# Squared-ReLU attention and a gated feed-forward on one core: a planned instruction order, 7-row loads, and crossbar transposes for batches 3 to 7

## The chip, the cores and the metric

The kernel runs on 1 core of a Trainium2 chip. The metric is device time in microseconds (us). A result here is the median of 4 to 7 executions of one kernel. Each kernel ran beside the kernel before, on the same chip in the same rounds; where two changed kernels of different rounds are compared, the kernel before differed by at most 0.4 us between them (505.1 to 505.5 us). TensorE is called PE, VectorE DVE, ScalarE ACT, GpSimd POOL, and the queue that issues stores and crossbar transposes SP. Tiles lie in SBUF; matmuls write theirs to PSUM, from where ACT or DVE copies them out (an eviction) before the PSUM tile can be used again. The granted clock is the share of the full TensorE clock that the profile shows.

## The reference, cut to what matters

```python
batch, n_heads, seq, head_dim = (8, 12, 448, 64)        # q, k, v in float32
n_tokens, d_model, d_ff = (3584, 768, 1536)

def _attn_ref(q, k, v):
    S = q.shape[2]
    scores = scale * np.matmul(q, k.transpose(0, 1, 3, 2))
    attn = np.maximum(scores, 0.0) ** 2 / S
    return np.matmul(attn, v)

def _moe_ref(x, w_gate, w_val, w_out):                  # x: the attention output, 3584 x 768
    gate = np.maximum(x @ w_gate, 0.0)
    val = x @ w_val
    return gate * val @ w_out
```

There is no softmax, so attention is two matmuls with a squared ReLU between them. The scores contract over the head dimension, so PE needs queries and keys with that dimension on the partitions; they arrive with the sequence there and have to be transposed.

## The kernel before

Loads go through POOL, which also casts to bf16. The 448 rows of a head are split into 384 in runs of 3 rows per partition and a tail of 64 single rows. PE transposes two heads at a time, and DVE copies the result out of PSUM:

```python
def load_batch(b, nsplit):                 # nsplit 3 for batches 0 and 1, else 1
    ...
    nc.gpsimd.dma_start(out=km[:, hs], in_=rows_main(k, b, hs))
    nc.gpsimd.dma_start(out=qm[:, hs], in_=rows_main(q, b, hs))
    nc.gpsimd.dma_start(out=tl[ko:ko + TAIL, hs], in_=rows_tail(k, b, hs))
    nc.gpsimd.dma_start(out=tl[qo:qo + TAIL, hs], in_=rows_tail(q, b, hs))
    nc.gpsimd.dma_start(out=vm[:, hs], in_=rows_main(v, b, hs))
    ...                                    # and four small loads of the tail of v

def transpose_pair(b, hp):
    t_ps = psum.tile([128, 2 * S], BF16, name="t_ps", tag="acc", bufs=4)
    for i in range(2 * NC + 1):
        for h2 in range(2):
            ...
            nc.tensor.transpose(t_ps[64 * h2:64 * h2 + 64, i * 128:(i + 1) * 128], blk, ident)
    qk_sb = tpool.tile([128, 2 * S], BF16, name="qk_sb")
    nc.vector.tensor_copy(qk_sb, t_ps)
```

Attention goes by groups of four heads, ten steps each: seven score steps `s`, one product with the values `pv` (of the group before), two transposes `t` (for the group after). Each score step is followed by a ReLU (144 of 168 on ACT, the others on DVE) and a square on DVE. The feed-forward of the batch before is a queue of units (6 or 12 matmuls each), and a running quota puts about one unit between every two attention steps:

```python
for i, s in enumerate(steps):
    s()
    if qd.g == 0 and qd.b > 0 and i == 3:
        ffn_queue.extend(ffn_units(qd.b - 1))
        per = len(ffn_queue) / (NQ * len(steps) - i - 1)
    acc += per
    while acc >= 1.0 and ffn_queue:
        ffn_queue.pop(0)()
        acc -= 1.0
```

The loads stand in the order batch 0, all gate and value weights, batch 1, output weights.

Of the kernel before, what the change touches and what calls it, by code (L numbers as in the profile page):

```python
# [8 lines left out]
FP32 = mybir.dt.float32  # L9
BF16 = mybir.dt.bfloat16  # L10
AF = mybir.ActivationFunctionType
ALU = mybir.AluOpType


@with_exitstack
def kernel(
# [10 lines left out]
    nc = tc.nc  # L27

# [5 lines left out]
    NC = S // 128  # L34
    MAIN = NC * 128
    TAIL = S - MAIN
    assert TAIL == 64 and D == 64
# [5 lines left out]
    WC = 256  # L43
# [6 lines left out]
    inp = ctx.enter_context(tc.tile_pool(name="inp", bufs=3))  # L50
    tpool = ctx.enter_context(tc.tile_pool(name="tpool", bufs=6))
    rpool = ctx.enter_context(tc.tile_pool(name="rpool", bufs=3))
    apool = ctx.enter_context(tc.tile_pool(name="apool", bufs=2))
    xpool = ctx.enter_context(tc.tile_pool(name="xpool", bufs=2))
    hpool = ctx.enter_context(tc.tile_pool(name="hpool", bufs=2))
# [3 lines left out]

    ident = const.tile([128, 128], BF16)  # L60
    make_identity(nc, ident)
# [3 lines left out]
    w_out_sb = wpool.tile([128, KF, d_model], BF16)  # L65

    def load_gv(c):
        cols = slice(c * WC, (c + 1) * WC)
        wg = moe_w_gate.rearrange("(kd p) f -> p kd f", p=128)
        wv = moe_w_val.rearrange("(kd p) f -> p kd f", p=128)  # L70
        nc.gpsimd.dma_start(out=w_gate_sb[c], in_=wg[:, :, cols])
        nc.gpsimd.dma_start(out=w_val_sb[c], in_=wv[:, :, cols])

    def load_out(c, n):
        wo = moe_w_out.rearrange("(kf p) m -> p kf m", p=128)
        s = slice(c * n, (c + 1) * n)
        nc.gpsimd.dma_start(out=w_out_sb[:, s], in_=wo[:, s])
# [3 lines left out]
    def rows_main(x, b, hs):  # L81
        return x[b, hs, 0:MAIN, :].rearrange("h (p t) d -> p h t d", t=NC)

    def rows_tail(x, b, hs):
        return x[b, hs, MAIN:S, :].rearrange("h p d -> p h d")

    batch = {}

    def q_first(b):
        return b % 2 == 0  # L90

    def load_batch(b, nsplit):
        qm = inp.tile([128, H, NC, D], BF16, name="qm")
        km = inp.tile([128, H, NC, D], BF16, name="km")
        tl = inp.tile([128, H, D], BF16, name="tl")
        vm = inp.tile([128, H, NC, D], BF16, name="vm")
        vt = inp.tile([128, NQ, 2, D], BF16, name="vt")
        qo, ko = (0, TAIL) if q_first(b) else (TAIL, 0)
        n = H // nsplit
        for i in range(nsplit):  # L100
            hs = slice(i * n, (i + 1) * n)
            nc.gpsimd.dma_start(out=km[:, hs], in_=rows_main(k, b, hs))  # L102
            nc.gpsimd.dma_start(out=qm[:, hs], in_=rows_main(q, b, hs))  # L103
            nc.gpsimd.dma_start(out=tl[ko:ko + TAIL, hs], in_=rows_tail(k, b, hs))  # L104
            nc.gpsimd.dma_start(out=tl[qo:qo + TAIL, hs], in_=rows_tail(q, b, hs))  # L105
            nc.gpsimd.dma_start(out=vm[:, hs], in_=rows_main(v, b, hs))  # L106

            gs = slice(i * n // 4, (i + 1) * n // 4)
            vq = v[b, hs, MAIN:S, :].rearrange("(g f) p d -> f p g d", f=4)
            nc.gpsimd.dma_start(out=vt[0:64, gs, 0], in_=vq[0])  # L110
            nc.gpsimd.dma_start(out=vt[0:64, gs, 1], in_=vq[3])
            nc.gpsimd.dma_start(out=vt[64:128, gs, 0], in_=vq[1])
            nc.gpsimd.dma_start(out=vt[64:128, gs, 1], in_=vq[2])
        batch[b] = (qm, km, tl, vm, vt)


    def col_offsets(b):
        if q_first(b):
            return 0, S
        return S, 0  # L120

    def transpose_pair(b, hp):
        qm, km, tl, vm, vt = batch[b]
        h0 = 2 * hp
        first, last = (qm, km) if q_first(b) else (km, qm)
        t_ps = psum.tile([128, 2 * S], BF16, name="t_ps", tag="acc", bufs=4)
        for i in range(2 * NC + 1):
            for h2 in range(2):
                h = h0 + h2
                blk = first[:, h, i, :] if i < NC else tl[:, h, :] if i == NC else last[:, h, i - NC - 1, :]  # L130
                nc.tensor.transpose(t_ps[64 * h2:64 * h2 + 64, i * 128:(i + 1) * 128], blk, ident)  # L131
        qk_sb = tpool.tile([128, 2 * S], BF16, name="qk_sb")
        nc.vector.tensor_copy(qk_sb, t_ps)  # L133
        return qk_sb


    def key_cols(b, c):
        if q_first(b):
            return S + TAIL + c * 128
        return c * 128  # L140

    def tail_cols(b):
        return S if q_first(b) else MAIN

    def q_cols(b):
        return slice(0, S) if q_first(b) else slice(S, 2 * S)

    def relu2(s_ps, dst, on_vec):
        src = s_ps[:, :, :S]
        r_sb = rpool.tile([128, 2, S], BF16, name="r_sb")  # L150
        if on_vec:
            nc.vector.tensor_scalar_max(r_sb, src, 0.0)  # L152
        else:
            nc.scalar.activation(r_sb, src, AF.Relu)  # L154
        nc.vector.tensor_tensor(dst, r_sb, r_sb, ALU.mult)  # L155

    xbuf = {}

    class Quad:
        def __init__(self, b, g):  # L160
            self.b, self.g = b, g
            self.qk = {}

        def t(self, j):
            self.qk[j] = transpose_pair(self.b, 2 * self.g + j)

        def s(self, i):
            b = self.b
            if i == 0:
                self.at = apool.tile([128, 7, 2, S], BF16, name="at")  # L170
            s_ps = psum.tile([128, 2, 512], FP32, name="s_ps", tag="s", bufs=2)
            qc = q_cols(b)
            if i < 6:
                qk = self.qk[i // NC]
                kc = key_cols(b, i % NC)
                for h2 in range(2):
                    p = slice(64 * h2, 64 * h2 + 64)
                    nc.tensor.matmul(s_ps[:, h2, :S], lhsT=qk[p, kc:kc + 128], rhs=qk[p, qc],  # L178
                                     start=True, stop=True)
            else:  # L180

                kc = tail_cols(b)
                for j, h2, half in ((0, 0, 0), (0, 1, 1), (1, 0, 1), (1, 1, 0)):
                    p = slice(64 * h2, 64 * h2 + 64)
                    o = slice(64 * half, 64 * half + 64)
                    nc.tensor.matmul(s_ps[o, h2, :S], lhsT=self.qk[j][p, kc:kc + TAIL],  # L186
                                     rhs=self.qk[j][p, qc], start=True, stop=True)
            relu2(s_ps, self.at[:, i], i == 2)

        def pv(self):  # L190
            b, g = self.b, self.g
            qm, km, tl, vm, vt = batch[b]
            x_ps = psum.tile([128, 2, 512], FP32, name="x_ps", tag="s", bufs=2)
            for j in range(2):
                for c in range(NC):
                    for h2 in range(2):
                        o = slice(64 * h2, 64 * h2 + 64)
                        nc.tensor.matmul(x_ps[o, j, :S], lhsT=vm[:, 4 * g + 2 * j + h2, c, :],  # L198
                                         rhs=self.at[:, 3 * j + c, h2, :],
                                         start=(c == 0), stop=False)  # L200
            for j, h2, half in ((0, 0, 0), (0, 1, 1), (1, 0, 1), (1, 1, 0)):
                p = slice(64 * half, 64 * half + 64)
                o = slice(64 * h2, 64 * h2 + 64)
                nc.tensor.matmul(x_ps[o, j, :S], lhsT=vt[p, g, j, :],  # L204
                                 rhs=self.at[p, 6, h2, :], start=False, stop=True)
            if g == 0:
                xbuf[b] = xpool.tile([128, KD, S], BF16, name="xT")
            nc.scalar.copy(xbuf[b][:, 2 * g:2 * g + 2, :], x_ps[:, :, :S])  # L208

    hbuf = {}  # L210

    def ffn_units(b):
        units = []
        if b % 2 == 0:
            hbuf[b // 2] = hpool.tile([128, KF, 2 * S], BF16, name="hT")
        hT = hbuf[b // 2]
        t0 = (b % 2) * S
        xT = xbuf[b]

        st = {}  # L220

        def g_unit(mf):
            def emit():
                c, o = divmod(mf * 128, WC)
                g_ps = psum.tile([128, 512], FP32, name="g_ps", tag="acc", bufs=4)[:, :S]
                for kd in range(KD):
                    nc.tensor.matmul(g_ps, lhsT=w_gate_sb[c][:, kd, o:o + 128], rhs=xT[:, kd, :],  # L227
                                     start=(kd == 0), stop=(kd == KD - 1))
                g_sb = gpool.tile([128, S], BF16, name="g_sb")
                nc.scalar.activation(g_sb, g_ps, AF.Relu)  # L230
                st[mf] = g_sb
            return emit
# [129 lines left out]
```

## Time and profile before

| | before |
|---|---|
| device time, median (range) | 505.3 us (504.5 to 505.86) |
| span of the profiled run | 502.9 us |
| PE busy | 470.9 us, 94% |
| PE busy in the first 50 us | 22.0 us |
| two batches, from the first output unit of one to that of the next but one | 116.4 us |
| interruptions of the feed-forward by attention in those two batches | 58 |

From the page of the kernel before: span, busy times, the rows of PE, its granted clock and the DMA engines in 40 slices (tenths), and the chain of waits that ended last.

```profile
span 502.9 us, 7712 instructions
...
PE 470.9 (94%) x3264; PEld 221.4 (44%) x3264; DVE 210.9 (42%) x336; ACT 224.1 (45%) x321; POOL 90.0 (18%) x130
...
PE   2842999999999999999999999999999999999997
...
PEclk9975999999999999999999999999999999999999
DMA  9999999975092423725092150010001200010002
...
PE 90%; DMA 5%; POOL 4%; issue 0%; ACT 0%; POOLq 0%
```

PE is full from the fifth slice to the last but one, and 90% of the chain that ended last is PE. Only the first 50 us have room. The timeline of PE shows the largest hole there (columns: start, duration, engine, line, operation, count, and in brackets the idle time before it and what ended it):

```profile
34.46 0.38 PE L186 MATMUL s_ps<-qk_sb 64*64 64x448 bf16 x4 [0.44 <-ACT r_sb L154]
47.25 0.85 PE L131 MATMUL t_ps<-ident,km 128*64 128x128 bf16 x12 [12.41 <-DMA km<-in_k_dram]
48.04 0.93 PE L227 MATMUL g_ps<-xT,wg_93 128*128 128x448 bf16 x2
```

PE waits 12.41 us for the keys of batch 1, which are queued behind all gate and value weights. The first feed-forward unit (L227) starts after that, at 48.0 us. The same view in the middle of the kernel:

```profile
229.07 1.31 PE L227 MATMUL g_ps<-xT,wg_93 128*128 128x448 bf16 x6
230.31 0.36 PE L178 MATMUL s_ps<-qk_sb 64*128 64x448 bf16 x2
230.61 1.31 PE L239 MATMUL v_ps<-xT,wv_99 128*128 128x448 bf16 x6
231.85 0.36 PE L178 MATMUL s_ps<-qk_sb 64*128 64x448 bf16 x2
232.15 1.31 PE L227 MATMUL g_ps<-xT,wg_94 128*128 128x448 bf16 x6
233.29 1.30 PE L239 MATMUL v_ps<-xT,wv_100 128*128 128x448 bf16 x6
234.52 0.36 PE L131 MATMUL t_ps<-ident,qm 128*64 128x128 bf16 x6
```

The starts are what to read. Unit L227 at 232.15 is followed by its like at 233.29, 1.14 us later. The unit before a score step holds PE 1.24 us (229.07 to 230.31) and the score step itself 0.30 us (230.31 to 230.61), where a second score step in a row takes 0.195 us. So an interruption of the feed-forward costs about 0.2 us, and there are 28 to 30 in a batch.

### The profile page before, as it was taken

To read this page: it belongs to the slowest core of one execution; us is meant where nothing else is said; L and a number is where in the kernel's file an instruction comes from. 1 tells how busy PE (TensorE), PEld (TensorE's weight loads), DVE (VectorE), ACT (ScalarE), POOL (GpSimd) and SP (SyncE) were. 2 spreads that over 40 slices of the span, in tenths; PEclk is the share of its full clock that TensorE was granted. 3 is DMA by queue.
4 is the path that set the end of the run, shared out by engine and by line. 5 is a ranking of instruction groups with operands and counts; after the bars stand their busy time and mean duration, and the time that the engine had idled before them with its cause. 6 is when DMAs were issued, how large, how long until landed. Compare 5 with 4: busy or idle time off the path is not lost.

```text
span 502.9 us, 7712 instructions
## 1 busy us (share of the span) xinstructions
PE 470.9 (94%) x3264; PEld 221.4 (44%) x3264; DVE 210.9 (42%) x336; ACT 224.1 (45%) x321; POOL 90.0 (18%) x130
## 2 busy tenths in 40 slices
PE   2842999999999999999999999999999999999997
PEld 1411444544445444454445444454445544455554
DVE  1750655335551454535452355515552255521210
ACT  2560555445453555445453454435553455443221
POOL 9944945420110202002020110000000000000000
PEclk9975999999999999999999999999999999999999
DMA  9999999975092423725092150010001200010002
GB/s 94 138 197 168 121 205 186 185 142 53 0 111 64 99 20 36 76 95 56 0 111 64 64 55 2 1 63 33 2 0 33 95 0 1 2 61 34 0 25 101
DMA packets 72161, 35.09 MB, mean 70 GB/s; under 512 B 57792, under 2 KB 68544, under 8 KB 72128
## 3 DMA queue, kind: packets, MB, share of 16 engines
q0 software_dynamic: 68032, 23.60, 42.0%
q1 hardware_dynamic: 4096, 11.01, 6.0%
q8 instruction: 25, 0.41, 0.3%
q14 instruction: 8, 0.07, 0.0%
HBM read 47.19 MB, written 11.01 MB: 116 GB/s over the span
## 4 chain that ended last, share of the span: by engine, by line
PE 90%; DMA 5%; POOL 4%; issue 0%; ACT 0%; POOLq 0%
PE g_ps L227 24%; PE v_ps L239 23%; PE o_ps L256 23%; PE s_ps L178 7%; PE x_ps L198 6%; PE t_ps L131 5%; DMA km<-in_k_dram 3%; DMA wg_95<-in_moe_w_gate_dram 2%; PE x_ps L204 1%; PE s_ps L186 1%; POOL km L102 0%; POOL vm L106 0%; POOL qm L103 0%; POOL tl L104 0%; POOL tl L105 0%; POOL vt L110 0%
## 5 line engine op out<-in xcount | busy, mean ns | idle before, releaser
L155 DVE TENSOR_TENSOR at<-r_sb 128x896 bf16<-128x896 bf16 x168 | 104.1, 624 | 173.5 <-ACT r_sb L154 173.0
L154 ACT ACTIVATE r_sb<-s_ps 128x896 bf16<-128x896 f32 x144 | 129.7, 917 | 64.4 <-PE s_ps L178 53.5
L256 PE MATMUL o_ps<-w_out_sb,hT 128*128 128x384 bf16 x672 | 115.8, 327 | 0.0
L230 ACT ACTIVATE g_sb<-g_ps 128x448 bf16<-128x448 f32 x96 | 52.3, 545 | 84.9 <-PE g_ps L227 84.9
L241 DVE TENSOR_TENSOR hT<-v_ps,g_sb 128x448 bf16<-128x448 f32 x96 | 59.6, 621 | 64.2 <-PE v_ps L239 64.2
L256 PEld LDWEIGHTS <-hT 128*128 128x128 bf16 x672 | 62.7, 98 | 44.8 <-issue 5.0
L260 ACT ACTIVATE o_sb<-o_ps 128x384 f32<-128x384 f32 x56 | 27.5, 491 | 82.5 <-PE o_ps L256 82.5
L178 PE MATMUL s_ps<-qk_sb 64*128 64x448 bf16 x288 | 52.9, 373 | 4.4 <-ACT r_sb L154 2.4
L133 DVE COPY qk_sb<-t_ps 128x896 bf16<-128x896 bf16 x48 | 29.6, 620 | 32.8 <-PE t_ps L131 32.8
L208 ACT CAST xT<-x_ps 128x896 bf16<-128x896 f32 x24 | 21.7, 906 | 43.0 <-PE x_ps L204 43.0
L178 PEld LDWEIGHTS <-qk_sb 64*128 64x128 bf16 x288 | 14.0, 93 | 50.4 <-issue 48.8
L198 PE MATMUL x_ps<-at,vm 128*64 128x448 bf16 x288 | 33.2, 366 | 0.4 <-ACT r_sb L154 0.4
L131 PE MATMUL t_ps<-ident,km 128*64 128x128 bf16 x288 | 19.2, 239 | 12.4 <-DMA km<-in_k_dram 12.4
L106 POOL DMA_DIRECT2D vm<-in_v_dram x12 | 11.0, 917 | 101.4 <-PE x_ps L198 69.7
L131 PE MATMUL t_ps<-ident,qm 128*64 128x128 bf16 x288 | 18.7, 238 | 9.4 <-DMA qm<-in_q_dram 9.4
L152 DVE TENSOR_SCALAR r_sb<-s_ps 128x896 bf16<-128x896 f32 x24 | 26.1, 1086 | 2.9 <-PE s_ps L178 2.9
L239 PE MATMUL v_ps<-xT,wv_99 128*128 128x448 bf16 x96 | 23.7, 358 | 0.0
L227 PE MATMUL g_ps<-xT,wg_93 128*128 128x448 bf16 x96 | 23.4, 363 | 0.0
L198 PEld LDWEIGHTS <-vm 128*64 128x64 bf16 x288 | 16.4, 112 | 14.9 <-issue 8.3
L131 PEld LDWEIGHTS <-km 128*64 128x64 bf16 x288 | 12.0, 119 | 21.7 <-DMA km<-in_k_dram 12.7
L239 PE MATMUL v_ps<-xT,wv_101 128*128 128x448 bf16 x96 | 20.9, 354 | 0.0
L227 PE MATMUL g_ps<-xT,wg_95 128*128 128x448 bf16 x96 | 20.9, 354 | 0.0
(55 smaller groups left out, 408.1 us busy)
## 6 DMA issues: line engine op xcount, KB each, us to landing
out_dram<-o_sb SPq DMA_DIRECT2D x24, 384.0 KB, 2.3
km<-in_k_dram POOLq DMA_DIRECT2D x6, 576.0 KB, 8.1
qm<-in_q_dram POOLq DMA_DIRECT2D x6, 576.0 KB, 9.2
vm<-in_v_dram POOLq DMA_DIRECT2D x6, 576.0 KB, 7.0
w_out_sb<-in_moe_w_out_dram POOLq DMA_DIRECT2D x4, 576.0 KB, 9.1
out_dram<-o_sb SPq DMA_DIRECT2D x8, 192.0 KB, 2.7
km<-in_k_dram POOLq DMA_DIRECT2D x6, 192.0 KB, 3.8
qm<-in_q_dram POOLq DMA_DIRECT2D x6, 192.0 KB, 4.2
```

Source lines behind the costliest of these rows:

```text
L131: nc.tensor.transpose(t_ps[64 * h2:64 * h2 + 64, i * 128:(i + 1) * 128], blk, ident)
L133: nc.vector.tensor_copy(qk_sb, t_ps)
L154: nc.scalar.activation(r_sb, src, AF.Relu)
L155: nc.vector.tensor_tensor(dst, r_sb, r_sb, ALU.mult)
L178: nc.tensor.matmul(s_ps[:, h2, :S], lhsT=qk[p, kc:kc + 128], rhs=qk[p, qc], start=True, stop=True)
L198: nc.tensor.matmul(x_ps[o, j, :S], lhsT=vm[:, 4 * g + 2 * j + h2, c, :], rhs=self.at[:, 3 * j + c, h2, :], start=(c == 0), stop=False)
L227: nc.tensor.matmul(g_ps, lhsT=w_gate_sb[c][:, kd, o:o + 128], rhs=xT[:, kd, :], start=(kd == 0), stop=(kd == KD - 1))
L230: nc.scalar.activation(g_sb, g_ps, AF.Relu)
L239: nc.tensor.matmul(v_ps, lhsT=w_val_sb[c][:, kd, o:o + 128], rhs=xT[:, kd, :], start=(kd == 0), stop=(kd == KD - 1))
L241: nc.vector.tensor_tensor(hT[:, mf, t0:t0 + S], v_ps, st[mf], ALU.mult)
L256: nc.tensor.matmul(o_ps, lhsT=hT[:, kf, ti * 128:(ti + 1) * 128], rhs=w_out_sb[:, kf, hf * OH:(hf + 1) * OH], start=(kf == 0), stop=(kf == ...
L260: nc.scalar.activation(out=o_sb[:, hf * OH:(hf + 1) * OH], in_=o_ps, func=AF.Copy, scale=float(out_scale))
```

## The change

It does four things. It loads q and k in runs of 7 rows (448 = 64 x 7) and v in runs of 4 and 3 of these, so the loads become fewer and longer. It gathers attention into bursts of two or three steps. It replaces the quota by a list schedule: a small planner with assumed durations picks, step by step, what can start next, which decides the order in which the operations are emitted, and it shares PSUM evictions between ACT and DVE. For batches 3 to 7 the transposes leave PE: DVE regroups q and k into pairs of heads (seven copies), and two crossbar DMAs on the SP queue transpose them from SBUF to SBUF. The planner cut to its core, and the parts that matter (lines joined and shortened; batch 0 has its steps in a slightly different order):

```diff
+    tc.manual_schedule(engines={ET.PE, ET.DVE, ET.Activation, ET.Pool, ET.SP})
+XBAR_FROM = 3
+class Op:                     # engines with assumed durations, dependencies, buffers, transfer time
+    def commit(self, op, s, e):                 # (of the planner)
+        self.t[e] = s + d
+        op.end = s + d
+        if op.xfer:
+            if e == "POOL":                     # loads: one queue, one transfer after the other
+                self.dmaq = max(self.dmaq, op.end + 1.0) + op.xfer
+                op.end = self.dmaq + 1.0
+            else:                               # stores and crossbar transposes on SP
+                op.end += 2.0 + op.xfer
+    ...
+    order = sorted(range(len(P.ops)), key=lambda i: (P.ops[i].start, i))
+    return [P.ops[i] for i in order]            # emitted in the order of planned starts
 
+    rows = lambda x: x[b, hs].rearrange("h (p t) d -> p h t d", t=NT)      # NT = 7
+    k_op = dma_in(lambda: tile_of("qk", NT)[64:128, hs], rows(k), 64 * n, 64 * n * 0.06 / 16, alloc=al)
+    q_op = dma_in(lambda: st.qk[0:64, hs], rows(q), 64 * n, 64 * n * 0.06 / 16)
+    v0, v1 = ...                                # the same with 0.045
 
+def transpose_batch(b):                         # batches 3 to 7
+    for s, t in enumerate(slot_order(b)):       # seven copies, on DVE
+        op = Op({"DVE": 0.28}, lambda s=s, t=t: emit_pair(s, t), deps=deps + perm[:1],
+                alloc=[pair] if s == 0 else [], reads=[st.buf])
+    for i in range(2):                          # q, then k: one crossbar DMA each, on SP
+        op = Op({"SP": 0.3}, lambda i=i: emit_x(i), deps=perm + xo[:1], ..., xfer=8.0)
 
+    for c in range(d_ff // WC):                 # batch 1 among the weights
+        load_gv(c)
+        if c % 2 == 0:
+            load_heads(1, 2 * c, 4)
 
+    nb += 1; att.append((qd.s(0), nb)); att.append((qd.s(1), nb))          # a burst
+    nb += 1; att.append((qd.s(2), nb)); PV()
+    nb += 1; att.append((qd.s(3), nb)); att.append((qd.s(4), nb)); T(n + 1)
+    nb += 1; att.append((qd.s(5), nb)); att.append((qd.s(6), nb))
```

For the loads of a whole batch (12 heads) the planner assumes 2.88 us each for k and q and 2.16 us for each half of v: 10.1 us of transfer in all, about 12 us with its two fixed microseconds. PSUM becomes four tiles of two banks that all work shares; there is one buffer `pair` for the regrouped heads and two for the transposed ones.

## The prediction

> **What bounds the kernel now.** TensorE. On the page PE is busy 94% of the 502.9 us span, and the chain of waits that ended last is 90% PE, with 5% DMA and 4% POOL at its start. By windows, PE is busy 100% from 50 us to the last matmul (about 499 us). Before that it loses some 28 us: in 0 to 50 us it is busy 22.0 us, much of that at a lowered clock (granted 0.77 and 0.50 in the two slices from 25 to 50 us, against 1.00 after). The largest hole, 34.8 to 47.3 us, waits for the keys of batch 1, which are queued behind all gate and value weights.
>
> After 50 us the timeline repeats with 116.4 us per two batches, 58.2 us each. Start to start, over four batches: feed-forward about 44 us per batch, scores 2.03 us and PV 1.57 us per group of four heads, transposes 0.545 us per pair of heads (3.3 us per batch). A lone score step takes 0.295 us, the second of two in a row 0.195 us; a gate or value unit takes 1.14 us after its like and 1.235 us where an attention step adjoins. So each interruption of the feed-forward costs about 0.2 us, and there are some 28 per batch. The Trainium skill (TensorEngine Tiling, Key Properties) says that changing the tiling mode drains the array; these differences agree.
>
> **What the change does.**
> 1. Transposes of batches 3 to 7 leave PE: 15 groups x 1.09 us = 16 us, all critical.
> 2. Attention comes in 4 bursts per group instead of about 9.5. My sum for a batch: feed-forward 42.2, scores 5.5, PV 4.7 = 52.4 us without transposes, 55.2 us with them, against 58.2. Five batches save 5.8, two save 3.0: about 35 us, step 1 included.
> 3. Start: fewer, longer DMA runs (12 loads for batch 0 instead of 27, issued at about 0.65 us each), batch 1 interleaved with the weights, evictions shared between ACT and DVE. A group in the start is bound by evictions: 8.8 us on ACT now; about 13.2 us of ACT and DVE work over two engines, so 6.6 us. Feed-forward of batch 0 should begin at about 33 us and PE stay full from there, instead of 47: about 15 us.
> 4. Added: seven DVE regroupings and two crossbar transposes of 0.69 MB per batch on the store queue. The skill (DMA: Bandwidth & Descriptors, Latency) gives 261 GB/s for transposing DMA, hence an estimate of 5 us per batch; nothing in this trace shows it. Against 52 us per batch and loads a batch ahead it is off the path.
>
> Sum: 505 - 35 - 15 = 455, plus about 4 us for imperfect packing.
>
> **Predicted: 459 us, 80% range 447 to 475.** Faster by over 2%: 0.95; within 2%: 0.03; slower: 0.02.
>
> **What would show it.** PE near 100% from about 33 us; no transposes on PE after batch 2; o-to-o period of two late batches near 105 us instead of 116.4; chain still about 90% PE; PE waits after 40 us under 8 us in total; crossbar landing in under 12 us.
>
> **What would make it wrong.** Crossbar transposes taking tens of microseconds, delaying scores or holding stores behind them on the same queue; PSUM tiles shared by both streams making PE wait on relu or square; the start still bound by weights or eviction; idle PE lowering the clock again; the plan's order blocking an in-order engine.

## The result

The change takes 476.16 us (475.33 to 477.61, 4 runs) against 505.3 us before. The ratio is 0.9427 (95% interval 0.9398 to 0.9457). All ratios here are the mean time of one kernel's fast runs over that of the other's of the same rounds, so not quite the ratio of the medians quoted. The direction and most of the mechanism were right, but 459 us was predicted with 475 us as the upper end.

The page of the change, the same rows:

```profile
span 475.9 us, 6835 instructions
...
PE 439.7 (92%) x2844; PEld 217.2 (46%) x2844; DVE 207.2 (44%) x343; ACT 216.8 (46%) x319; POOL 45.6 (10%) x68
...
PE   3769999996999999996999969999999999999995
...
PEclk9899999997999999998999988999999999999999
DMA  9999999997317800793027940079001300021013
...
PE 74%; DMA 17%; DVE 2%; ACT 2%; POOL 2%; issue 2%; SPq 0%; ACTq 0%; DVEq 0%; POOLq 0%
```

PE is full earlier. But there are now dents in its row and in its clock in the middle of the kernel (slices 10, 19 and 24), and the chain that ended last is 17% DMA and only 74% PE; by lines, 13% are loads of queries and 4% key transposes. Three stops of PE explain the dents:

```profile
PE ps L501 <- DVE hT L517: 4.6, 1, 4.6
PE ps L405 <- DVE hT L517: 4.5, 1, 4.5
PE ps L309 <- DVE hT L517: 4.0, 1, 4.0
```

Each time PE waited, by this view, for a DVE multiplication (L517, gate times value, which frees PSUM). The second stop in full: first PE, then DVE, then POOL and SP, which issue the DMAs.

```profile
216.43 1.30 PE L501 MATMUL ps<-xT,wg_99 128*128 128x448 bf16 x6
222.20 0.56 PE L405 MATMUL ps<-qT,kT 64*128 64x448 bf16 x2 [4.47 <-DVE hT L517]
222.69 2.45 PE L451 MATMUL ps<-at,vv 128*64 128x448 bf16 x12
...
225.38 1.31 PE L511 MATMUL ps<-xT,wv_105 128*128 128x448 bf16 x6
```
```profile
212.08 0.63 DVE L517 TENSOR_TENSOR hT<-ps,g_sb 128x448 bf16<-128x448 f32 x1 [0.74 <-ACT g_sb L506]
219.64 1.97 DVE L350 COPY pair<-qk 128x768 bf16<-128x768 bf16 x7 [6.94 <-DMA qk<-in_q_dram]
221.53 0.62 DVE L517 TENSOR_TENSOR hT<-ps,g_sb 128x448 bf16<-128x448 f32 x1
```
```profile
199.66 1.50 POOL L232 DMA_DIRECT2D vv<-in_v_dram  x2 [48.31 <-PE ps L456]
...
201.87 0.80 POOL L232 DMA_DIRECT2D qk<-in_q_dram  x1
```
```profile
199.57 4.14 SPq L362 DMA_TRANSPOSE kT<-pair  x1
```

DVE finishes L517 at 212.7 us. The next instruction in its order is the first regrouping (L350) of batch 6, whose queries are still on their way, so it stands still for 6.94 us. Behind it in the same queue is the multiplication that PE needs. PE still does two score steps and three feed-forward units; its next score step then needs a PSUM tile that this multiplication frees, and PE stops for 4.47 us. The Trainium skill ("TensorE: Matmul & The Clock Gate", Architectural detail, engine queue depths) says ACT and DVE are strict FIFO; the trace agrees: L517 starts the moment the copies end. The copies were in no hurry: the first crossbar transpose of this batch started at 245.4 us, 23.8 us after the last of them. The chain of waits says the same from the other end (start, duration, what):

```profile
199.66 1.31 POOL vv L232 x2
...
201.87 17.70 DMA qk<-in_q_dram
...
219.64 1.97 DVE pair L350 x7
221.61 0.54 DVE hT L517
...
222.20 0.56 PE ps L405 x2
```

The third stop is like the second: DVE waits 6.85 us for queries of batch 7. At the first, the view names the key transpose of batch 3, which was still reading the single buffer `pair` (issued at 91.7 us, landed 18.9 us later, at 110.6). But the queries of batch 4 had landed only at 110.0 us (issued at 89.15 us, 20.8 us to landing), so without the busy buffer DVE would have waited only 0.6 us less:

```profile
91.73 10.41 SPq L362 DMA_TRANSPOSE kT<-pair  x1
110.72 1.97 DVE L350 COPY pair<-qk 128x768 bf16<-128x768 bf16 x7 [6.65 <-DMA kT<-pair]
```

After the stop at 222 us PE runs slowly. The windows of that stop and of what follows give the granted clock as the third number from the end:

```profile
217.70:222.20 4.50, 0.03 (x1) 0.05 (x1) 2.56 (x9) 0.55 (x1) 0.00 (x0) 0.94 0.06 9
222.20:226.40 4.20, 4.20 (x24) 1.70 (x24) 2.17 (x4) 1.81 (x2) 0.00 (x0) 0.66 0.00 0
```

PE gets 0.66 of its clock over the next 4.2 us, so the PV product at 222.69 took 2.45 us where 1.33 us is usual. After the other two stops the clock was 0.51 for 5.6 us and 0.50 for 5.7 us. That agrees with the skill's page just named (Part 1: an idle window of about 3.4 us halves the clock). The three stops cost 3.99 + 4.47 + 4.62 = 13.1 us, and the slow clock after them 5.6 x 0.49 + 4.2 x 0.34 + 5.7 x 0.50 = 7.0 us.

Where nothing stops, the two late batches from 308.4 to 414.0 us took 105.6 us. The prediction had named 105 us as the sign that the bursts and the crossbar work.

### The profile page after: what moved, and what is told of

It is laid out like the page before. It is cut to its first block, busy times and chain, and to the rows that moved or that the text cites. A ratio compares the mean times of both kernels' runs of the same rounds, so it can differ in the third digit from the quotient of the medians.

```text
span 475.9 us, 6835 instructions
## 1 busy us (share of the span) xinstructions
PE 439.7 (92%) x2844; PEld 217.2 (46%) x2844; DVE 207.2 (44%) x343; ACT 216.8 (46%) x319; POOL 45.6 (10%) x68
## 3 DMA queue, kind: packets, MB, share of 16 engines
q0 software_dynamic: 37856, 24.38, 35.8%
q1 hardware_dynamic: 31680, 17.90, 19.8%
## 4 chain that ended last, share of the span: by engine, by line
PE 74%; DMA 17%; DVE 2%; ACT 2%; POOL 2%; issue 2%; SPq 0%; ACTq 0%; DVEq 0%; POOLq 0%
PE ps L542 21%; PE ps L501 20%; PE ps L511 20%; DMA qk<-in_q_dram 13%; PE ps L451 5%; PE ps L405 5%; DMA kT<-pair 4%; PE ps L456 1%; DVE pair L350 1%; PE ps L309 1%; ACT r_sb L426 1%; PE ps L411 1%; POOL qk L232 1%; POOL vv L232 1%; DVE hT L517 1%
## 5 line engine op out<-in xcount | busy, mean ns | idle before, releaser
L426 ACT ACTIVATE r_sb<-ps 128x896 bf16<-128x896 f32 x134 | 117.5, 925 | 8.3 <-PE ps L405 8.3
L506 ACT ACTIVATE g_sb<-ps 128x448 bf16<-128x448 f32 x96 | 52.3, 545 | 138.7 <-PE ps L511 110.0
L517 DVE TENSOR_TENSOR hT<-ps,g_sb 128x448 bf16<-128x448 f32 x96 | 59.8, 624 | 116.5 <-ACT g_sb L506 103.2
L550 ACT ACTIVATE o_sb<-ps 128x384 f32<-128x384 f32 x56 | 25.0, 490 | 79.2 <-PE ps L542 76.2
L542 PE MATMUL ps<-wo_109,hT 128*128 128x384 bf16 x336 | 59.3, 326 | 0.8 <-ACT r_sb L426 0.8
L542 PE MATMUL ps<-wo_110,hT 128*128 128x384 bf16 x336 | 59.2, 326 | 0.3
L428 DVE TENSOR_SCALAR r_sb<-ps 128x896 bf16<-128x896 f32 x34 | 37.1, 1090 | 47.0 <-PE ps L405 38.3
L451 PE MATMUL ps<-at,vv 128*64 128x448 bf16 x288 | 33.2, 368 | 0.4 <-ACT r_sb L426 0.4
L405 PE MATMUL ps<-qT,kT 64*128 64x448 bf16 x180 | 27.1, 362 | 4.5 <-DVE hT L517 4.5
L470 ACT CAST xT<-ps 128x896 bf16<-128x896 f32 x23 | 21.0, 913 | 11.5 <-PE ps L456 11.5
L501 PE MATMUL ps<-xT,wg_99 128*128 128x448 bf16 x96 | 21.9, 366 | 4.6 <-DVE hT L517 4.6
L309 PE MATMUL ps<-ident,qk 128*64 128x128 bf16 x252 | 12.4, 271 | 14.9 <-DMA qk<-in_q_dram 9.8
L501 PE MATMUL ps<-xT,wg_100 128*128 128x448 bf16 x96 | 22.2, 370 | 0.0
L511 PE MATMUL ps<-xT,wv_105 128*128 128x448 bf16 x96 | 22.0, 367 | 0.0
L511 PE MATMUL ps<-xT,wv_106 128*128 128x448 bf16 x96 | 21.6, 362 | 0.1
L501 PE MATMUL ps<-xT,wg_97 128*128 128x448 bf16 x96 | 21.6, 363 | 0.0
L451 PEld LDWEIGHTS <-vv 128*64 128x64 bf16 x288 | 14.9, 112 | 13.8 <-issue 7.0
L511 PE MATMUL ps<-xT,wv_107 128*128 128x448 bf16 x96 | 20.8, 352 | 0.2
L501 PE MATMUL ps<-xT,wg_98 128*128 128x448 bf16 x96 | 20.8, 353 | 0.0
## 6 DMA issues: line engine op xcount, KB each, us to landing
vv<-in_v_dram POOLq DMA_DIRECT2D x12, 384.0 KB, 10.1
qk<-in_q_dram POOLq DMA_DIRECT2D x6, 672.0 KB, 19.2
```

The lines of the kernel that those rows point to most:

```text
L405: nc.tensor.matmul(s_ps[:, h2, :S], lhsT=k_of(h2, key_off(b) + (i % NC) * 128, 128), rhs=q_of(h2), start=True, stop=True)
L426: nc.scalar.activation(loc["r"], loc["s"][:, :, :S], AF.Relu)
L428: nc.vector.tensor_scalar_max(loc["r"], loc["s"][:, :, :S], 0.0)
L451: nc.tensor.matmul(x_ps[o, j, :S], lhsT=st.vv[:, 4 * g + 2 * j + h2, 1 + c, :], rhs=at[:, NC * j + c, h2, :], start=(c == 0), stop=False)
L501: nc.tensor.matmul(loc["g"], lhsT=w_gate_sb[c][:, kd, o:o + 128], rhs=st.xT[:, kd, :], start=(kd == 0), stop=(kd == KD - 1))
L506: nc.scalar.activation(loc["gs"], loc["g"], AF.Relu)
```

## The experiments

My theory after reading the trace (A): the plan's order puts the regroupings in DVE's queue before their data (at the first stop, their buffer too) are there, and an in-order queue makes everything behind them wait. Rival (B): the crossbar traffic, the shared PSUM tiles or the clock cost the time, wherever the regroupings stand. Both regrouping shifts, the kernel without crossbar and the bursts alone ran on one chip together, beside the kernel before (505.1 us).

### The regroupings 12 us later

The sort key of the emission order gets a shift for the regroupings and their crossbar transposes alone. The instruction orders of PE, ACT and POOL were compared with those of the change and are identical.

```diff
-    order = sorted(range(len(P.ops)), key=lambda i: (P.ops[i].start, i))
+    order = sorted(range(len(P.ops)), key=lambda i: (P.ops[i].start + P.ops[i].late, i))
+    # op.late = 12.0 for the seven regroupings and two transposes of each batch, else 0.0
```

> Edit: the seven regroupings and two crossbar transposes of each batch are put 12 us later in the order of their engines (DVE and SP); the orders of PE, ACT and POOL stay instruction for instruction the same. Theory A (the plan lets DVE reach the regroupings before the loads have landed; DVE works in order, so the products behind them wait, PSUM stays full, PE stops three times for 4.0 to 4.6 us and then runs some microseconds at half clock): the three stops vanish, PE idle after 40 us falls from 14.7 us to under 2 us, time 454 to 459 us. Rival B (crossbar traffic, shared PSUM tiles or the clock itself cost the time, wherever the regroupings stand): 473 to 478 us.

Measured: 457.93 us (457.56 to 458.59), ratio to before 0.9065 (0.905 to 0.908). These are all the waits of PE after 40 us; the timeline of DVE at batch 6 shows a regrouping without a bracket, so without a wait:

```profile
PE ps L411 <- DVE hT L517: 1.2, 2, 0.6
PE ps L542 <- ACT r_sb L426: 0.8, 4, 0.2
```
```profile
218.68 0.63 DVE L432 TENSOR_TENSOR at<-r_sb 128x896 bf16<-128x896 bf16 x1 [0.18 <-ACT r_sb L426]
219.22 0.62 DVE L350 COPY pair<-qk 128x768 bf16<-128x768 bf16 x2
219.75 0.62 DVE L432 TENSOR_TENSOR at<-r_sb 128x896 bf16<-128x896 bf16 x1
```

The three stops are gone, and 18.2 us with them. The transfers became no faster: the median landing of a batch's queries is 20.8 us here and 19.2 us in the change, that of the query and key transposes 12.0 and 15.8 us here and 7.0 and 11.9 us in the change. From the first output unit of batch 0 to that of batch 4 this kernel takes 214.6 us and the change 234.9 us; the difference of 20.3 us is, to 0.2 us, the 13.1 us of stops and 7.0 us of slow clock found above. B falls: nothing but the place of the regroupings and of their transposes changed, and the run on POOL below leaves the transposes in their place.

### The regroupings 6 us earlier

The same edit with -6.0, as a dose in the other direction.

> Edit: the regroupings and crossbar transposes stand 6 us earlier in the orders of DVE and SP than in the change; PE, ACT and POOL keep their orders. Theory A: the three stops of PE get longer, by up to 6 us each, and the regroupings that were just in time (batches 3, 5) begin to stop PE too: 488 to 505 us. Rival B: 473 to 479 us, no change.

Measured: 489.99 us (488.89 to 493.56), ratio 0.9712 (0.9673 to 0.9752), 13.8 us slower than the change. DVE now stands still before the regroupings of all five batches (5.6, 8.6, 7.7, 10.1 and 7.3 us; in the change 0.3, 6.7, 2.2, 6.9 and 6.9 us). Counting stops of over 0.9 us, PE now stops for all five batches (1.3, 5.6, 4.9, 5.7 and 4.5 us; in the change only for batches 4, 6 and 7, 4.0, 4.5 and 4.6 us). The sum grows from 13.1 to 22.0 us, 8.9 of the 13.8 us, and the mean granted clock from 100 to 300 us falls from 0.96 to 0.94. So the stops follow the position of the regroupings, though not by the full 6 us each, and not at batch 7.

### The regroupings on POOL

Same place in the plan, another engine. PE, ACT and SP keep the orders of the change, and DVE only loses the copies.

```diff
-            nc.vector.tensor_copy(box["p"][:, :, s], st.qk[:, :, t, :].rearrange(...))
+            nc.gpsimd.tensor_copy(box["p"][:, :, s], st.qk[:, :, t, :].rearrange(...))
```

> Edit: the seven regroupings of each batch are issued on POOL instead of DVE, at the same place of the plan; PE, ACT and SP keep the orders of the change, DVE only loses the 35 regroupings. Theory A (waiting regroupings at the head of an in-order queue stop what stands behind them): behind them on POOL stand only loads with slack, so the three stops of PE vanish although loads and crossbar transposes are as slow as before; 456 to 461 us. Rival B (the slow loads and crossbar transfers themselves hold PE): 472 to 478 us.

Measured: 458.03 us (456.27 to 459.14), ratio 0.9057 (0.9033 to 0.9082). The data of batch 6 come as late as before (19.8 us after the issue of v, 19.9 us in the change), and each copy takes 2.6 times as long (915 ns on POOL, 355 ns on DVE), but what stands behind them on POOL is a load with slack. (Before these copies the view names no releaser for the wait, only "issue".)

```profile
193.32 0.78 POOL L232 DMA_DIRECT2D qk<-in_k_dram  x1
194.06 0.80 POOL L232 DMA_DIRECT2D qk<-in_q_dram  x1
211.62 5.65 POOL L350 COPY pair<-qk 128x768 bf16<-128x768 bf16 x7 [16.77 <-issue]
```

So it is not the waiting of the regroupings that costs time, but whom they keep waiting.

### No crossbar

```diff
-XBAR_FROM = 3
+XBAR_FROM = 8
```

> Edit: the crossbar is used for no batch (the constant 3 becomes 8); plan, 7-row loads and bursts stay. Theory A: no regroupings, so no stop of PE after 40 us above 1 us; 15 more groups of transposes on PE at about 0.95 us each, 14 us; time 467 to 473 us, so faster than the change as it is. Rival B (the stops come from the plan or the shared PSUM tiles): stops remain, 485 us or more. Also read: if the loads of a whole batch land within 12 us here (17 to 19 us with the crossbar), the crossbar traffic stretched them; if still 17 us or more, their own shape did.

Measured: 468.64 us (467.42 to 470.49), ratio 0.9281 (0.9256 to 0.9305). PE waited 0.2 us in all after 40 us. As shipped, the crossbar part made the kernel 7.5 us slower (476.16 against 468.64); with its regroupings in the right place it makes it 10.7 us faster (457.93 against 468.64). Two batches take 110.8 us here and 106.0 us with the crossbar undisturbed.

The expectation also wanted to read from this run whether the crossbar stretches the loads. It can't: without the crossbar the q and k loads wait for PE's transposes instead, so they no longer go out together with the v loads, and the landing times (6.6 and 9.4 us for k and q) answer another question. Within the trace of the change the loads of v, k and q of a whole batch went out together three times after 100 us. From the issue of v to the regroupings' data it took 15.3 us at 148 us, with no transpose near, and 19.9 us at 199 and at 260 us, each time with a key transpose issued shortly before. In the run with the earlier regroupings it was 15.5 us with no transpose near and 17.8 us with a key transpose issued 6 us before. The skill ("DMA: Bandwidth & Descriptors", Issuing engines are not separate DMA queues) says that transfers started from different engines run on the same 16 DMA engines and interleave, which fits. I have seen this side by side and have not isolated it. Either way the planner's 12 us was too short.

### The bursts alone, in the kernel before

Here `both` calls its arguments one after the other, and `t` holds the two transposes.

```diff
-        for i in range(7):
-            out_steps.append(lambda i=i: qd.s(i))
-            if i == 2 and prv is not None:
-                out_steps.append(prv.pv)
-            if nxt is not None and i in (3, 5):
-                out_steps.append(lambda j=(i - 3) // 2: nxt.t(j))
+        out_steps.append(both(s[0], s[1]))
+        out_steps.append(both(s[2], prv.pv) if prv is not None else s[2])
+        out_steps.append(both(s[3], s[4], *t))
+        out_steps.append(both(s[5], s[6]))
 ...
-            if qd.g == 0 and qd.b > 0 and i == 3:
+            if qd.g == 0 and qd.b > 0 and i == 1:
```

> Edit to the kernel before alone: its ten attention steps per group of four heads are emitted as four bursts (two score steps; one score step and PV; two score steps and both transposes; two score steps), nothing else. Theory A (each interruption of the feed-forward costs about 0.2 us of PE): some 17 of 28 interruptions per batch go, about 3 us per batch over seven batches, 484 to 488 us. Rival (the gain of the change comes from its start and from the crossbar, not from merging): 503 to 506 us.

Measured: 486.97 us (486.32 to 488.2), ratio 0.9643 (0.9628 to 0.9659). Two batches take 110.9 us instead of 116.4 us with 26 interruptions instead of 58, so one costs 5.5 / 32 = 0.17 us. That is the two-batch time of the plan without crossbar (110.8 us): in the steady part the planner gains nothing over this edit of a few lines. The 18.3 us between this kernel and that one lie in the start. PE waits for loads in the first 60 us fall from 22.1 to 9.7 us, its waits for ACT and DVE do not (5.5 and 5.7 us). In the 7.7 us after its hole of 12.4 us this kernel has 0.70 of the clock, about 2.3 us more; the other has its full clock (1.00) in the 7.7 us after its first unit. The first feed-forward unit begins at 48.4 us here and at 35.8 us there, and the first output unit of batch 0 at 92.4 and 72.8 us.

### The bursts taken apart, in the planned kernel

Each attention step of batches 1 to 7 gets a burst number of its own (`nb += 1` before every step) on top of the regroupings 12 us later.

> Edit to the kernel with the later regroupings: each attention step is made a burst of its own for the plan (about 24 interruptions of the feed-forward per batch instead of 11). Theory (an interruption costs about 0.2 us of PE, whatever wrote the plan): 13 more in each of seven batches, 473 to 480 us. Rival (the plan gains by better packing, not by fewer interruptions): 457 to 461 us.

Measured: 472.59 us (471.44 to 473.62), ratio 0.9341 (0.9318 to 0.9364). It is 0.4 us under the expected range, and the reason is in the count: the planner still put steps together, so there were 38 interruptions per two batches, not 48, against 22. They cost 110.4 - 106.0 = 4.4 us, 0.27 us each; 1.8 us of that is PE waiting for ACT and DVE, and the rest is 0.16 us each. The rival, that the plan packs better however it cuts, falls.

### The start: batch 1 loaded earlier

In the change PE's order has the transposes of batch 1, heads 4 to 7, ahead of the first feed-forward unit (L501), and they wait for their queries:

```profile
30.84 0.55 PE L405 MATMUL ps<-qk_sb 64*128 64x448 bf16 x4
34.14 1.71 PE L309 MATMUL ps<-ident,qk 128*64 128x128 bf16 x28 [2.75 <-DMA qk<-in_q_dram]
35.78 2.07 PE L501 MATMUL ps<-xT,wg_97 128*128 128x448 bf16 x6
```

```diff
-        if c % 2 == 0:
-            load_heads(1, 2 * c, 4)
+        if c < 3:
+            load_heads(1, 4 * c, 4)
```

> Edit to the kernel with the later regroupings: in the start the heads 4 to 7 and 8 to 11 of batch 1 are loaded after the second and third pair of weight chunks instead of after the third and fifth. Theory (the transposes of batch 1, heads 4 to 7, stand before the first feed-forward unit in the order of PE and wait 2.75 us for their queries): the first feed-forward unit starts at about 33 us instead of 35.8, 454.5 to 456.5 us. Rival (evictions bound the start): 457 to 459 us.

Measured, with the regroupings 12 us later: 455.17 us (454.97 to 455.31), ratio 0.9004 (0.899 to 0.9017). The first unit starts at 31.9 us. Part of that is given back at 70.3 us, where PE now waits 2.28 us for queries of batch 2, which moved behind. It is the same fault in small: an order made for data that come later than assumed.

### The planner told longer durations

No shift here. The loads of batches 4 to 7 are planned twice as long, the others 1.1 times as long, the transposes 14 us instead of 8, with the load order above.

```diff
+    SL = lambda b: 2.0 if b > XBAR_FROM else 1.1
-                    ... 64 * n * 0.06 / 16 ...           (k, q; v likewise with 0.045)
+                    ... SL(b) * 64 * n * 0.06 / 16 ...
-                    reads=[pair], xfer=8.0)
+                    reads=[pair], xfer=14.0)
```

> Edit to the change itself: no shift; the planner is given longer durations (loads of batches 4 to 7 twice as long, the others 1.1 times, crossbar transposes 14 us instead of 8) and the load order of the run before. Theory A: a plan with true durations puts the regroupings where their data are; no stop of PE over 1 us after 40 us, 454 to 458 us. Rival: still 465 us or more.

Measured: 455.1 us (454.63 to 455.33), ratio 0.9001 (0.8988 to 0.9015), and no stop of PE over 0.7 us after 40 us. The planner was not at fault, its numbers were. The new numbers are longer ones on the safe side, not the measured ones put in one by one, and the load order changed along with them. This version and the one before it beat both kernels and can't be told apart; this one needs no correction by hand.

### The crossbar from batch 2

The last kernel with `XBAR_FROM = 2`. By the rule above, the loads of batch 3 are then planned twice as long too.

> Edit to the kernel with longer planned durations and the other load order: the crossbar also takes batch 2. Theory (a batch moved off PE is worth about 2.1 us, as 468.6 against 457.9 us for five batches shows, if its data come in time): 452 to 454.5 us. Rival (batch 2 is loaded in the start, beside the weights, so its regroupings hold DVE or its scores wait for the crossbar): 456 us or more, with stops of PE between 65 and 110 us.

Measured: 464.57 us (463.72 to 465.54), ratio 0.919 (0.917 to 0.9209): the rival. PE stops at two places:

```profile
71.68 0.59 PE L412 MATMUL ps<-qk_sb 64*64 64x448 bf16 x4 [2.88 <-DVE hT L518]
72.20 13.26 PE L543 MATMUL ps<-wo,hT 128*128 128x384 bf16 x72
94.25 1.30 PE L406 MATMUL ps<-qT,kT 64*128 64x448 bf16 x6 [8.79 <-DMA kT<-pair]
```

At 71.7 us it is DVE again, held by regroupings that wait 4.2 us for queries loaded beside the weights. At 94.3 us the scores themselves wait 8.79 us for the key transpose. That transpose was issued at 87.6 us, after six stores in front of it on SP (81.4 to 87.5 us).

## Why the prediction was wrong

The bound and the direction held, and so did the sum of the gains: 18.1 us for the bursts, 10.7 us for the crossbar and, by difference, 18.3 us for the start make 47.1 us, against 50 us in the prediction. What failed is one step: point 4 with its sum, "Against 52 us per batch and loads a batch ahead it is off the path" and "plus about 4 us for imperfect packing". The loads were far ahead of the scores but not of the copies: at the second stop DVE reached the copies 10.8 us after the issue of the queries, which took 17.7 us. Measured as the change against the same instructions with the regroupings and their transposes later, the loss was 18.2 us. The prediction without its 4 us would have been 455 us, and the kernel without the loss takes 457.93 us. That these come so near is partly luck: the start gave 3.3 us more than forecast, bursts and transposes together 6.2 us less.

- **PE bounds the kernel, in the start it waits for loads:** right, by the chain before and by every run.
- **Transposes of batches 3 to 7, 16 us:** smaller. Shown are 10.7 us. I had costed a group at 1.09 us in the old order, where its two transposes are two interruptions of about 0.2 us that the bursts take away anyway (an estimate, not tested alone); the batch sums of my point 2 had allowed for that (55.2 against 52.4 us, so 14 us for five batches) and were nearer.
- **Bursts:** right in kind and nearly in size. Two batches with transposes were to save 3.0 us each, and the burst edit alone saved 2.75 us each and 18.1 us in all. The sign named for late batches, 105 us for two, was 105.6 us.
- **Start, 15 us:** about right, and mostly by the loads. The forecast gave three reasons and the runs do not separate them, but the waits of PE for loads fell by 12.4 us and those for ACT and DVE did not, so nothing shows the gain from shared evictions. The first feed-forward unit came at 35.8 us instead of the 33 us named, 2.75 us of it a wait for one load. All that separates the burst edit from the plan without crossbar is 18.3 us, some 2.3 us of it the clock.
- **Crossbar:** right that its own duration is off the path where it is placed well, wrong in its size. The 5 us per batch for both transposes came from the skill's 261 GB/s ("DMA: Bandwidth & Descriptors", Latency); landing took 7.0 us (queries) and 11.9 us (keys) in the median and 18.9 us at worst, against under 12 us as the sign named. The worst one held the `pair` buffer at the first stop of PE, but only 0.6 us longer than the next queries took to land.
- **Regroupings:** the miss. The prediction lists the copies and weighs what is added by its duration (DVE's share turned out small, 35 copies of 355 ns, 12.4 us in all). It does not ask where these copies stand in DVE's queue and what they wait for. "The plan's order blocking an in-order engine" was on my list of what could go wrong, but I gave it no size, although everything for it was in the diff: the assumed 10.1 us for the loads of a batch, on an engine that also frees PSUM for PE. PE waits after 40 us were to stay under 8 us; the three stops alone were 13.1 us, all of them with late queries, one with a late key transpose as well.
- **Idle PE lowering the clock:** on the list as well, and real: 7.0 us on top of the 13.1 us of the stops themselves.

## What to carry to other kernels

An instruction on an in-order engine costs its duration plus all that waits behind it while its data are missing, so put work that waits for a DMA late, or on an engine with nothing urgent behind it. A static schedule is as good as its assumed durations: measure transfers in the trace under the load they will meet and feed them back. Here longer durations and a better load order took 476.16 us to 455.1 us, of which the load order alone gave 2.8 us in the hand-shifted kernel. Before crediting a rewrite to its largest part, try its smallest: grouping the attention steps, an edit of a few lines, alone gave 18.1 us where the whole change as shipped gave 29 us.

## What the Trainium skill lacked or had wrong

- "DMA: Bandwidth & Descriptors" (Latency and other measured facts) gives 261 GB/s for transposing DMA. Here a transpose of 0.69 MB from 64 partitions, SBUF to SBUF, landed in 6.5 us at best (0.69 MB / 6.5 us = 106 GB/s, fixed costs included) and in 18.9 us at worst beside loads of a batch. The page has no figure for this mix of traffic.
- "TensorEngine Tiling (Array Packing)" (Key Properties) says that a change of the tiling mode drains the array and gives no cost. Here an interruption of 128-row matmuls by attention steps and the return cost 0.16 to 0.17 us by the two burst experiments; they do not separate the drain from whatever else the switch costs.
- "TensorE: Matmul & The Clock Gate" has the strict FIFO of DVE and the clock after an idle window, both as seen here. No page follows a wait from one engine's queue to the clock of PE: here 13.1 us of stops behind waiting copies on DVE cost 7.0 us more by the clock.
